# A Fourier layer with a two-layer MLP: one batch's middle stage scheduled over 42 slots in place of 44

## Chip, cores, metric

One core of a Trainium2 chip. The time is that of the device for one execution, in microseconds (us); lower is better. PE is the matrix engine, DVE the vector engine, ACT the scalar engine, SPq the queue in which the sync engine issues transfers; PEld in the profile is PE's loading of weights, POOL the GpSimd engine. A "look" is one profiled execution. A transfer has "landed" when the last update of its semaphore is recorded.

## The reference, cut

```python
def _attn_ref(x, w_r, w_i, b_r, b_i):            # x: 8 x 3008 x 256
    X = np.fft.rfft(x, axis=1)
    Xr, Xi = X.real, X.imag
    Yr = Xr @ w_r - Xi @ w_i + b_r
    Yi = Xr @ w_i + Xi @ w_r + b_i
    # soft threshold of both by 0.01
    Yr = np.sign(Yr) * np.maximum(np.abs(Yr) - 0.01, 0.0)
    Yi = np.sign(Yi) * np.maximum(np.abs(Yi) - 0.01, 0.0)
    return np.fft.irfft(Yr + 1j * Yi, n=3008, axis=1)

def _moe_ref(x, w_in, w_out, s, b):              # x: 24064 x 256, hidden 2048
    r = np.maximum(x @ w_in, 0.0)
    return (s * (r * r) + b) @ w_out
```

## The kernel before

The transform of length 3008 = 94 x 32 is done as matmuls: a first DFT over 94 ("s1", the row DFT), a second over 32, the complex mix, the inverse over 32 (these three are "s23"), and a last DFT over 94 ("s4"). Batch 0 goes alone. Each later batch is woven into the MLP of earlier ones: the MLP runs slot by slot, and a plan says which unit of the transform is issued in which slot.

```python
    def schedule(start, span, units):
        for i, u in enumerate(units):
            plan.setdefault(start + (i * span) // len(units), []).append(u)
    ...
    schedule(24, 44, s23_units(1))               # 44 units: one to a slot, 24 to 67
    schedule(mark[1] - 14, 12, s4_units(1))      # mark[1] = 96: slots 82 to 93
    for b in range(2, B):
        s0, s1, s2 = mark[b - 2], mark[b - 1], mark[b]
        p = s1 - s0
        schedule(s0 + 40, p - 48, s1_units(b))   # batch 2: slots 40, 43, ... 85
        ...
    for ti in range(ti_n + 1):
        nxt = second_mms(ti - 1) if ti else []
        per_slot = -(-len(nxt) // MC)
        for mc in range(MC):                     # a slot
            if ti < ti_n:
                for u in plan.pop(ti * MC + mc, []):
                    u()
                first_mm(ti, mc)                 # 2 matmuls of 512 columns into psh (L761)
            for u in nxt[mc * per_slot : (mc + 1) * per_slot]:
                u()                              # 4 matmuls of 256 columns into psa (L832)
```

All transform units share two PSUM banks, the pool `psf`:

```python
        def fwd_unit(i):     # second DFT: 4 matmuls (L598), copy to xf, sum of its halves (L604)
        def sum_unit(h):     # 4 matmuls on that sum (L613)
        def mix_unit(i):     # 4 matmuls (L627), then 4 DVE operations, first L632 reads the bank
        def inv_unit(i):     # 2 matmuls (L657), copy to v
            ...
            if i % 2 == 1:   # two units' v go to DRAM
                nc.sync.dma_start(out=vd[2 * i - 2 : 2 * i + 2]..., in_=v)      # L666
            if i == H - 1:   # the whole comes back turned: vs, in two halves
                ...
                    nc.sync.dma_start(out=t..., in_=vv[...])                     # L673
        # s1 unit: one matmul of 512 columns (L562); s4 unit: 5 matmuls of 96 (L710) on vs
```

The built order is that of a scheduler, which may move a unit within or just over its slot. Copies out of PSUM go to DVE (line L164) or ACT (L160) by a running total of their loads. In the profile `u` and `us` are the row DFT's result on its way to DRAM and back, `xf` the second DFT's, `yt` the last DFT's; `rt` and `gt` are the MLP's hidden values before and after squaring, `ost` is an output tile.

## Time and profile before

| | before |
|---|---|
| three runs, us | 852.54, 853.90, 854.17 |
| span of the profiled run | 851.2 us |
| PE busy | 834.2 us, 98% |
| DVE, ACT busy | 82%, 76% |
| PE clock granted | 1.000 |

The lines of this profile stand in the prediction below. A line of the order of time reads: start in us, duration in us, engine, source line, operation, output <- inputs, shape, how many in a row, and in brackets how long the engine was idle before it and what ended that.

A **stall** is the time from one matmul's start to the next one's, less 0.4225 ns for each column of the first (the rate of an undisturbed stream, where 512 columns take 0.216 us); only stalls over 0.1 us are counted. The **main stretch** runs from the first to the last L832 matmul, some 787 us; it leaves out the start, where inputs are loaded. It was 788.58 us in this profile. The first expectations below count from the first L598 matmul of batch 1 instead (779.6 us in this profile); where that matmul isn't moved, the main stretch is 8.95 us longer.

### The profile page before, as it was taken

The numbers are of one execution on the slowest core, as the hardware profiler recorded it, in microseconds if no ns is written. First come the engines' busy times: TensorE is split into PE (matmuls) and PEld (weight loads), VectorE is DVE, ScalarE is ACT, GpSimd is POOL, SyncE is SP. The second block draws the span as 40 slices with busy tenths as digits, with TensorE's granted clock in tenths as the row PEclk, the third lists the DMA queues.
The fourth block names the chain that finished last, engine by engine and source line by source line (L and its number), as shares of the span: only waits on it lengthen the run. The fifth ranks groups of instructions, "written<-read, shape, count | busy, mean of one in ns | idle before, by whom it ended". The sixth has DMA issues, their size and how long they took to land.

```text
span 851.2 us, 17087 instructions
## 1 busy us (share of the span) xinstructions
PE 834.2 (98%) x6645; PEld 598.4 (70%) x6645; DVE 697.7 (82%) x1025; ACT 642.9 (76%) x858; POOL 47.2 (6%) x72
## 2 busy tenths in 40 slices
PE   7899999999999999999999999999999999999997
PEld 6757776777677766777667776777667777766765
DVE  6898987888878887888878888888977888776674
ACT  5897787788778887787777887787877787766673
POOL 5421000000000000000000000000000000000000
PEclk9999999999999999999999999999999999999999
DMA  7937457424672357324662247613354233411111
GB/s 168 157 100 161 105 139 178 120 76 98 159 200 60 90 150 191 113 78 99 165 176 75 75 106 192 178 38 94 101 156 118 57 83 98 112 33 38 38 44 50
DMA packets 105458, 95.07 MB, mean 112 GB/s; under 512 B 9510, under 2 KB 97578, under 8 KB 104034
## 3 DMA queue, kind: packets, MB, share of 16 engines
q1 hardware_dynamic: 98930, 79.57, 32.5%
q0 software_dynamic: 6448, 14.42, 10.5%
q8 instruction: 52, 0.85, 0.4%
q14 instruction: 28, 0.23, 0.1%
HBM read 52.54 MB, written 46.66 MB: 117 GB/s over the span
## 4 chain that ended last, share of the span: by engine, by line
PE 87%; DVE 4%; ACT 3%; DMA 3%; issue 1%; POOL 0%; DVEq 0%; ACTq 0%; SPq 0%; POOLq 0%
PE psa L832 36%; PE psh L761 35%; PE psf L627 4%; PE psf L562 2%; PE psf L598 2%; PE psf L613 2%; PE psf L710 2%; PE psf L657 2%; DVE gt L775 1%; ACT rt L768 1%; DMA x<-in_x_dram 1%; DMA vs<-vd 1%; DMA vd<-v 1%; PE psh L410 1%; DMA out_dram<-ost 0%
## 5 line engine op out<-in xcount | busy, mean ns | idle before, releaser
L768 ACT ACTIVATE rt<-psh 128x1024 f32<-128x1024 f32 (+2 forms) x384 | 387.1, 1009 | 116.8 <-PE psh L761 115.6
L775 DVE TENSOR_TENSOR gt<-rt 128x1024 f16<-128x1024 f32 (+2 forms) x323 | 386.6, 1200 | 98.4 <-ACT rt L768 97.9
L832 PE MATMUL psa<-w_out_t,gt 128*128 128x256 f16 (+1 forms) x3024 | 454.5, 272 | 0.1
L832 PEld LDWEIGHTS <-gt 128*128 128x128 f16 (+1 forms) x3024 | 301.0, 101 | 187.5 <-issue 1.7
L761 PE MATMUL psh<-yt,w_in 128*128 128x512 f16 (+1 forms) x1344 | 396.6, 378 | 0.3 <-ACT rt L768 0.3
L761 PEld LDWEIGHTS <-w_in 128*128 128x128 f16 x1536 | 142.7, 98 | 27.7 <-issue 2.7
L842 DVE SCALAR_TENSOR_TENSOR ost<-psa,s_bc,bias_bc 128x512 f32<-128x512 f32 (+2 forms) x97 | 71.1, 733 | 8.3 <-PE psa L832 6.9
L772 ACT ACTIVATE gt<-rt 128x1024 f16<-128x1024 f32 (+2 forms) x61 | 64.0, 1050 | 0.9
L632 DVE TENSOR_TENSOR ring<-psf,s 128x512 f16<-128x512 f32 x84 | 57.5, 685 | 4.3 <-PE psf L627 4.0
L160 ACT CAST v<-psf 128x512 f16<-128x512 f32 x78 | 45.4, 582 | 19.4 <-PE psf L657 19.4
L160 ACT CAST xf<-psf 128x512 f16<-128x512 f32 x83 | 48.6, 586 | 11.1 <-PE psf L598 11.1
L160 ACT CAST u<-psf 96x512 f16<-96x512 f32 x81 | 46.9, 581 | 11.9 <-PE psf L562 11.6
L761 PE MATMUL psh<-tail,w_in 128*128 128x512 f16 (+1 forms) x192 | 52.1, 353 | 0.0
L627 PE MATMUL psf<-W_g,xf 128*128 128x256 f16 x336 | 50.4, 273 | 0.0
L160 ACT CAST yt<-psf 128x480 f16<-128x480 f32 (+2 forms) x74 | 37.4, 517 | 14.7 <-PE psf L710 14.7
L189 POOL DMA_DIRECT2D x<-in_x_dram x36 | 18.9, 531 | 430.9 <-PE psf L562 430.0
L562 PE MATMUL psf<-x,A_t 94*96 94x512 f16 x104 | 39.6, 381 | 1.9 <-ACT yt L160 0.5
L638 DVE TENSOR_TENSOR ring<-ring,high 128x512 f16<-128x512 f16 x84 | 35.5, 423 | 2.1
L639 DVE TENSOR_TENSOR ring<-ring 128x512 f16<-128x512 f16 x84 | 35.5, 423 | 2.0
L637 DVE TENSOR_TENSOR ring<-ring,low 128x512 f16<-128x512 f16 x84 | 35.4, 422 | 1.6
L627 PEld LDWEIGHTS <-xf 128*128 128x128 f16 x336 | 32.9, 98 | 3.7
L710 PE MATMUL psf<-C_t,vs 96*128 96x96 f16 x448 | 32.9, 205 | 0.9 <-DMA vs<-vd 0.9
(89 smaller groups left out, 495.8 us busy)
## 6 DMA issues: line engine op xcount, KB each, us to landing
out_dram<-ost SPq DMA_DIRECT2D x152, 128.0 KB
ud<-u SPq DMA_DIRECT2D x28, 384.0 KB
us<-ud SPq DMA_DIRECT2D x28, 384.0 KB
vd<-v SPq DMA_DIRECT2D x42, 256.0 KB
vs<-vd SPq DMA_DIRECT2D x14, 768.0 KB
x<-in_x_dram POOLq DMA_DIRECT2D x28, 376.0 KB, 6.0
ring<-ring SPq DMA_DIRECT2D x280, 32.0 KB
out_dram<-ost SPq DMA_DIRECT2D x16, 120.0 KB
```

The lines of the kernel that those rows point to most:

```text
L160: return None, nc.scalar.copy(out=dst, in_=src)
L562: nc.tensor.matmul(ps[0:96, :], A_t[0:N1, :], x16[(b, c)][0:N1, j * D : (j + 2) * D], start=True, stop=True,)
L627: nc.tensor.matmul(ps[:, r, :], xt[:, 2 - r, dc], W_g[:, dc, r], start=(dc == 0), stop=(dc == DC - 1),)
L632: nc.vector.tensor_tensor(out=t, in0=ps, in1=hold[i // 2][:, i % 2].unsqueeze(1).to_broadcast([P, 2, D]), op=ALU.add,)
L638: nc.vector.tensor_tensor(out=m, in0=m, in1=high, op=ALU.min)
L710: nc.tensor.matmul(ps[:, j * 96 : (j + 1) * 96], vs[(b, h)][:, k, ec * P : (ec + 1) * P], C_t, start=True, stop=True,)
L761: nc.tensor.matmul(o, w_in_t[dc][:, mc * P : (mc + 1) * P], r, start=(dc == 0), stop=(dc == DC - 1),)
L768: nc.scalar.activation(out=rt[:, :, 0:w], in_=ps[:, :, 0:w], func=AF.Relu)
L772: nc.scalar.activation(out=gt[:, :, 0:w], in_=rt[:, :, 0:w], func=AF.Square)
L775: nc.vector.tensor_tensor(out=gt[:, :, 0:w], in0=rt[:, :, 0:w], in1=rt[:, :, 0:w], op=ALU.mult)
L832: nc.tensor.matmul(ps[0:size, h, :], gts[(ti, mc // 2)][:, mc % 2, sub * size : (sub + 1) * size], w_out_t[:, mc, :], start=(mc == 0), sto ...
L842: nc.vector.scalar_tensor_tensor(out=ost[0:size, 0:k], in0=ps[0:size, 0:k], scalar=s_bc[0:size], in1=bias_bc[0:size, 0:k], op0=ALU.mult, o ...
```

## The change

The intent: let the last inverse of batch 1 come two slots earlier, so that its result is back from DRAM when the last DFT needs it.

```diff
-    schedule(24, 44, s23_units(1))
+    schedule(24, 42, s23_units(1))
     schedule(mark[1] - 14, 12, s4_units(1))
```

## The prediction

> **What bounds the kernel now.** I read the page first, then the sum of PE's waits, then the order of time around the two places that the change touches. The page and its row of slices:
>
> ```profile
> PE 834.2 (98%) x6645; PEld 598.4 (70%) x6645; DVE 697.7 (82%) x1025; ACT 642.9 (76%) x858; POOL 47.2 (6%) x72
> PE   7899999999999999999999999999999999999997
> PEclk9999999999999999999999999999999999999999
> ```
>
> PE is busy for 98% of the span at full clock, and only the first slices and the last fall short. All PE idle time is 851.2 - 834.2 = 17.0 us. The view of waits, restricted to PE from 60 to 140 us, which holds all of batch 1's second DFT, mix and inverse, has one entry:
>
> ```profile
> PE psf L710 <- DMA vs<-vd: 0.9, 1, 0.9
> ```
>
> That is the first matmul of the last DFT of batch 1, which needs `vs`, reloaded from DRAM after the inverse has stored `vd`. The order of time there, first PE, then the queue of the sync engine:
>
> ```profile
> 133.90 0.57 PE L761 MATMUL psh<-yt,w_in 128*128 128x480 f16 x2
> 134.30 0.60 PE L832 MATMUL psa<-w_out_t,gt 128*128 128x256 f16 x4
> 135.79 0.60 PE L710 MATMUL psf<-C_t,vs 96*128 96x96 f16 x10 [0.89 <-DMA vs<-vd]
> ...
> 118.91 1.86 SPq L787 DMA_DIRECT2D out_dram<-ost  x2
> 120.87 3.21 SPq L666 DMA_DIRECT2D vd<-v  x2
> 129.12 0.79 SPq L673 DMA_DIRECT2D vs<-vd  x2
> ```
>
> Without the wait the last DFT would have come at 134.30 + 0.44 = 134.74, so it costs 135.79 - 134.74 = 1.05 us of PE's stream (0.89 is what remains after the modelled end of the matmuls before it). The last inverse unit is issued at 120.15, so the way from it to the landed `vs` is 135.75 - 120.15 = 15.6 us, and PE offers 134.74 - 120.15 = 14.6 us of other work. The shortfall is the wait.
>
> How long is a slot, the unit of the schedule? It is two matmuls of 512 columns into `psh` and four of 256 into `psa`. From 67.22 to 68.09 below, such a block takes 0.87 us: 0.43 for the pair, 0.44 for the four. A DFT unit (four of 128) takes 0.22, a sum or mix unit 0.44, an inverse unit 0.22.
>
> ```profile
> 67.00 0.39 PE L598 MATMUL psf<-F_t,us 128*128 128x128 f16 x4
> 67.22 0.59 PE L761 MATMUL psh<-yt,w_in 128*128 128x512 f16 x2
> 67.23 0.74 DVE L842 SCALAR_TENSOR_TENSOR ost<-psa,s_bc,bias_bc 128x512 f32<-128x512 f32 x1
> 67.66 0.60 PE L832 MATMUL psa<-w_out_t,gt 128*128 128x256 f16 x4
> 67.89 1.21 DVE L775 TENSOR_TENSOR gt<-rt 128x1024 f16<-128x1024 f32 x1
> 68.09 0.39 PE L598 MATMUL psf<-F_t,us 128*128 128x128 f16 x4
> 69.02 0.48 DVE L604 TENSOR_TENSOR xf<-xf 128x256 f16<-128x256 f16 x2
> 69.36 0.61 PE L613 MATMUL psf<-W_t,xf 128*128 128x256 f16 x4
> ```
>
> This is the head of the stage: DFT 0, one block, DFT 1, one block, sum 0. The sum unit needs both `xf` additions of the vector engine (L604), and these stand behind a `gt` that runs to 69.10. So it starts at 69.36, already 0.18 us after PE was ready (68.75 + 0.43).
>
> **What the Trainium skill says.** "TensorE: Matmul & The Clock Gate", section "Back-to-back issue gap", gives N / 2.4 + 2.5 ns between warm matmuls: 216 ns at 512 columns, 109 at 256. The trace agrees: 0.43 us a pair and 0.44 us four. So PE has no slack inside a block, and only waits can be won. "DMA: Bandwidth & Descriptors", section "Two DMAs through the same engine are not ordered", has the issuing engine wait for the completion of a write before it issues a read of the same bytes. The trace agrees: the sync queue sits from 124.1 to 129.1 us between the store of `vd` and the load of `vs` (the view of that queue's waits has 4.9 us), so an earlier last inverse moves the whole chain. "DVE: scalar operands, raw-bit mode, write accounting and state across instructions", section "Flops that outlive an instruction", calls the vector engine's queue one in-order queue. The trace agrees: the two additions start at 69.02 together, right behind `gt`, though the first `xf` had been copied by 68.27.
>
> **The change part by part.** There are 44 units (12 DFT, 6 sum, 12 mix, 12 inverse, 2 empty). Over 44 slots they lie one to a slot, 24 to 67. Over 42 slots they lie in 24 to 65, and two slots hold two: slot 24 (DFT 0 and 1) and slot 45 (inverse 2 and DFT 9). No instruction is added or removed on PE. The evacuation helper keeps running totals and sends a few copies elsewhere: over the program the order of instructions shows `u` copies on the vector engine 27 in place of 23, `yt` and `gt` squarings three fewer, and the scalar engine takes two more squarings. From about a third of the program on both engines' orders are the same to the end. So the tail is not touched.
>
> Part 1, the `vs` wait. The last inverse comes two slots earlier, so 2 x 0.87 = 1.74 us more of other work lies behind it: 14.6 + 1.7 = 16.3 us against the 15.6 needed. The wait goes, with 0.7 us to spare: -1.05 us. In the sync queue the store of the last-but-one `v` now also stands ahead of two stores of `ost` (1.86 us), which gives a little more room.
>
> Part 2, the head. DFT 0 and 1 are now issued at 67.00 and 67.22. In the built order sum 0 follows after the 512-column pair and three of the four 256-column matmuls: PE is ready at 67.44 + 0.43 + 0.33 = 68.20. The vector engine's order there is unchanged (`ost`, `gt`, two additions), and neither `ost` nor `gt` depends on a DFT unit, so the additions still come at 69.02 and sum 0 at 69.36. The stall is 69.36 - 68.20 = 1.16 us in place of 0.18: +0.98 us.
>
> Part 3, waits for the two `psf` banks in 91 to 121 us. I compared start to start of all matmuls with 0.4225 ns a column, and found six stalls above 0.1 us there: 0.12 + 0.31 + 0.19 + 0.19 + 0.26 + 0.31, together about 1.4 us. The pattern behind the 0.31 at 94.33 is a mix, then a block, an inverse, and at once a third user of `psf`, whose bank the vector engine still reads (L632 from 93.60 to 94.28). In the new order this comes back once, as DFT 9 behind inverse 2 in slot 45. The burst at the end (inverse 8 to 11 with row-DFT units of batch 2 between) has one such unit in place of two. I put the new sum at about 1.1 us: -0.3 us, with an uncertainty of 0.5.
>
> Sum: -1.05 + 0.98 - 0.3 = about -0.4 us, so 853.9 - 0.4 = 853.5 us.
>
> **The rivals.** First, the head's stall is smaller than I say, if the vector engine reaches the additions sooner, or if the scalar engine does not queue. For it: a wait of 1 us is unusual in this kernel after 60 us. Against it: the order of the vector engine is the same and its times there come from `ost` and `gt`. Then the gain is near -1.3, and the time 852.6. Second, a new wait takes the place of the removed one: the vector engine is busy for 14.2 of 15 us from 85 to 100 us, and the same work in two slots less delays `psf` banks. For it: that share of 0.95 is the highest of all stretches that I read. Against it: the head's stall gives the vector engine back a microsecond first. Each lost bank costs 0.3 us, so three of them make it 854.4. Third, the transfer is not hidden: the DMA engines are busy for 0.97 to 1.09 of the time from 130 to 136 us, and a stronger overlap with the load of `x` at 126.99 would stretch `vs`. Then part of the 1.05 stays, and the time is 854.0 to 854.6.
>
> **Range and chances.** All terms are near 1 us and two of them cancel. Their spread is some 0.7 us and the three runs of before differ by 1.6 us (852.54 to 854.17). I take 852.0 to 855.2 for 8 in 10. A change of 2% is 17 us, more than all waits of the stage together, and as much as all idle time of PE: faster 0.01, slower 0.01, within 2% 0.98.
>
> **What would show it right or wrong.** Step 1: no wait of PE L710 for `vs` near 135 us, and the load issued earlier relative to the first last-DFT matmul. Step 2: a gap of about 1 us before the first L613, with the two additions at 69.0 behind `gt`. Step 3: the stalls of L562, L598 and L657 for banks between 90 and 122 us adding up to 0.6 to 1.6 us. After 150 us the two traces should run parallel. If the gap at 69 us is missing, step 2 is wrong; if the later batches differ by more than 0.5 us, the moved copies matter more than I allow.

## The result

In the first job the changed kernel took 851.91 us (median of 6, 851.16 to 853.40), the one before 854.90 us (6 runs, 852.54 to 856.12). The ratio is 0.9969, with a 95% interval of 0.9952 to 0.9986. A ratio is the mean time of one kernel's fast runs over that of the other's of the same rounds, so not quite the ratio of these medians. By the 2% rule it is the same time; the small gain is clear of the noise in this job. The profiled run's span is 849.4 us, 1.8 less than before.

The page's busy times after the change:

```profile
PE 835.0 (98%) x6645; PEld 600.5 (71%) x6645; DVE 697.0 (82%) x1027; ACT 643.2 (76%) x856; POOL 46.6 (5%) x72
```

The view of PE's waits from 60 to 145 us has no entry any more. The order of time around the store of `vd` and the load of `vs`, after the change:

```profile
116.27 0.37 SPq L666 DMA_DIRECT2D vd<-v  x1
117.83 1.32 SPq L787 DMA_DIRECT2D out_dram<-ost  x2
119.60 0.78 SPq L666 DMA_DIRECT2D vd<-v  x1
125.11 0.80 SPq L673 DMA_DIRECT2D vs<-vd  x2
...
133.48 0.97 ACT L768 ACTIVATE rt<-psh 128x960 f32<-128x960 f32 x1 [0.66 <-PE psh L761]
133.71 0.59 PE L710 MATMUL psf<-C_t,vs 96*128 96x96 f16 x10
134.34 1.02 ACT L160 CAST yt<-psf 128x480 f16<-128x480 f32 x2
134.55 0.27 PE L832 MATMUL psa<-w_out_t,gt 128*128 128x256 f16 x1
134.95 0.38 PE L562 MATMUL psf<-x,A_t 94*96 94x512 f16 x1
```

The load of `vs` is issued at 125.1 us instead of 129.1, and its first half has landed at 130.64, by the record of its semaphore; PE comes to it at 133.71 and finds it there. The next thing to see is at 134.95: PE could have started this L562 at 134.66, but its `psf` bank is one that the copies of `yt` are just emptying, a stall of 0.29 us. ACT was still at L768 when the first five L710 were done. In the profile before, PE stood still for a microsecond in front of L710, ACT had ended its L768 meanwhile, and the copies were not late:

```profile
136.21 1.02 ACT L160 CAST yt<-psf 128x480 f16<-128x480 f32 x2 [0.74 <-PE psf L710]
```

Part of the wait that went has come back as a wait for a bank. The head of the stage, after the change:

```profile
66.71 0.61 PE L598 MATMUL psf<-F_t,us 128*128 128x128 f16 x8
67.16 0.59 PE L761 MATMUL psh<-yt,w_in 128*128 128x512 f16 x2
67.59 0.60 PE L832 MATMUL psa<-w_out_t,gt 128*128 128x256 f16 x4
67.60 1.21 DVE L775 TENSOR_TENSOR gt<-rt 128x1024 f16<-128x1024 f32 x1
68.03 0.59 PE L761 MATMUL psh<-yt,w_in 128*128 128x512 f16 x2
68.46 0.49 PE L832 MATMUL psa<-w_out_t,gt 128*128 128x256 f16 x3
68.73 0.48 DVE L604 TENSOR_TENSOR xf<-xf 128x256 f16<-128x256 f16 x2
69.07 0.61 PE L613 MATMUL psf<-W_t,xf 128*128 128x256 f16 x4
```

Both DFT units are issued together (x8), then a whole block and most of a second one, and only then the sum unit L613. The stall there is 69.07 - (68.46 + 0.33) = 0.28 us, not the 1.16 predicted.

Stalls in the two profiles, us:

| place | before | after |
|---|---|---|
| head (first L613) | 0.18 | 0.29 |
| `psf` banks, 72 us to the last DFT | 1.37 | 0.51 |
| first L710, wait for `vs` | 1.05 | 0 |
| last DFT of batch 1, behind it | 0 | 0.58 |
| everything later | 3.18 | 3.03 |
| main stretch | 788.58 | 787.10 |

The stalls fall by 1.37 us together; the rest of the 1.48 us lies in differences below 0.1 us each.

From 350 us on, the L832 matmuls of the two traces lie the same distance apart, 1.76 to 1.77 us, to the end: the copies that moved between DVE and ACT (the last of them near 244 us) cost nothing later. Of this distance 0.29 us arose before the first L832, where both kernels are the same.

### The profile page after: what moved, and what is told of

Same layout as the page of the kernel before. It is cut to its first block, busy times and chain, and to the rows that moved or that the text cites. A ratio compares the mean times of both kernels' runs of the same rounds, so it can differ in the third digit from the quotient of the medians.

```text
span 849.4 us, 17085 instructions
## 1 busy us (share of the span) xinstructions
PE 835.0 (98%) x6645; PEld 600.5 (71%) x6645; DVE 697.0 (82%) x1027; ACT 643.2 (76%) x856; POOL 46.6 (5%) x72
## 4 chain that ended last, share of the span: by engine, by line
PE 88%; DVE 4%; ACT 3%; DMA 2%; issue 1%; POOL 0%; SPq 0%; DVEq 0%; ACTq 0%; POOLq 0%
PE psa L832 36%; PE psh L761 36%; PE psf L627 4%; PE psf L562 2%; PE psf L613 2%; PE psf L598 2%; PE psf L657 2%; PE psf L710 2%; ACT rt L768 1%; DVE gt L775 1%; DMA x<-in_x_dram 1%; DMA out_dram<-ost 1%; PE psh L410 1%; ACT yt L160 0%; ACT vs L160 0%
## 5 line engine op out<-in xcount | busy, mean ns | idle before, releaser
L768 ACT ACTIVATE rt<-psh 128x1024 f32<-128x1024 f32 (+2 forms) x384 | 387.1, 1009 | 119.1 <-PE psh L761 117.7
L832 PE MATMUL psa<-w_out_t,gt 128*128 128x256 f16 (+1 forms) x3024 | 454.3, 272 | 0.1
L832 PEld LDWEIGHTS <-gt 128*128 128x128 f16 (+1 forms) x3024 | 300.9, 101 | 187.2 <-issue 1.7
L772 ACT ACTIVATE gt<-rt 128x1024 f16<-128x1024 f32 (+2 forms) x63 | 66.2, 1050 | 1.0
L160 ACT CAST u<-psf 96x512 f16<-96x512 f32 x77 | 44.5, 580 | 11.0 <-PE psf L562 10.7
L562 PE MATMUL psf<-x,A_t 94*96 94x512 f16 x104 | 39.7, 381 | 1.7 <-ACT yt L160 0.5
L710 PE MATMUL psf<-C_t,vs 96*128 96x96 f16 x448 | 33.0, 205 | 0.1
```

The lines of the kernel that those rows point to most:

```text
L160: return None, nc.scalar.copy(out=dst, in_=src)
L562: nc.tensor.matmul(ps[0:96, :], A_t[0:N1, :], x16[(b, c)][0:N1, j * D : (j + 2) * D], start=True, stop=True,)
L710: nc.tensor.matmul(ps[:, j * 96 : (j + 1) * 96], vs[(b, h)][:, k, ec * P : (ec + 1) * P], C_t, start=True, stop=True,)
L768: nc.scalar.activation(out=rt[:, :, 0:w], in_=ps[:, :, 0:w], func=AF.Relu)
L772: nc.scalar.activation(out=gt[:, :, 0:w], in_=rt[:, :, 0:w], func=AF.Square)
L832: nc.tensor.matmul(ps[0:size, h, :], gts[(ti, mc // 2)][:, mc % 2, sub * size : (sub + 1) * size], w_out_t[:, mc, :], start=(mc == 0), sto ...
```

## The experiments

Three theories after the result. A: the gain is in the kernel, as the table has it, and every entry repeats. B: the waits scatter from run to run. C: the measured 0.3% is mostly scatter in the start, where inputs are loaded.

### The kernel before, once more

No edit; five rounds against itself.

> The kernel before, unchanged, against itself. Theory A (the difference is in the kernel: the vs wait and waits for psf banks): ratio 1.000 within 0.002, and in the trace the stretch from the first L598 matmul of batch 1 to the last L832 matmul is again 779.6 us within 0.2, with the vs wait of 0.9 us and bank waits in the same places. Rival B (waits scatter from run to run): the vs wait or the bank waits between 90 and 122 us move by more than 0.3 us. Rival C (the measured 2.6 us is mostly scatter outside of this stretch): the span differs by up to 2 us from 851.2 with the stretch unchanged, by the loads before 20 us.

Measured: 853.52 us (852.02 to 855.83), ratio 1.0011 (0.9995 to 1.0028); main stretch 787.72 us. All six bank stalls are where they were, and sum to 1.37 us again. But the wait for `vs` is gone:

```profile
120.28 1.28 SPq L666 DMA_DIRECT2D vd<-v  x2
127.25 0.79 SPq L673 DMA_DIRECT2D vs<-vd  x2
134.68 0.59 PE L710 MATMUL psf<-C_t,vs 96*128 96x96 f16 x10
```

Sync queue and PE, as above. Here the first half of `vs` landed at 134.59, and PE came at 134.68: just in time, in the very program that had waited 1.05 us. So theory A is wrong for this entry and right for the banks, and the wait for `vs` is a race that PE sometimes loses. I had built on one execution. With this I went on with theory A2: what the order fixes repeats, and the `vs` wait is drawn anew in each execution.

### The last DFT one slot later

```diff
-    schedule(mark[1] - 14, 12, s4_units(1))
+    schedule(mark[1] - 13, 12, s4_units(1))
```

> Before, with the last DFT of batch 1 one slot later and its units left where they were (44 slots): only the vs wait is touched. Theory A: the wait falls by one block, from 1.05 to about 0.2 us, and some 0.3 us come back as a bank wait in the last DFT; stretch 779.6 - 0.6 = 779.0 us, bank waits in 90 to 122 us as before (1.4 us). Rival B (the vs wait alone is what the change gains): the stretch falls by 0.85. Rival D (the wait does not matter): 779.6.

Measured: 852.46 us (851.02 to 852.90), ratio 0.9988 (0.9974 to 1.0002); main stretch 787.63 us, bank stalls 1.38, `vs` stall 0.62 us. It could not tell the theories apart: one slot of more time, and yet 0.62 us of wait, because in this execution `vs` landed 16.2 us after the last inverse (15.6 in the first profile, 14.5 in the second). Nor did it touch the `vs` wait alone, as I had expected: the stalls after 150 us fell from 3.18 to 2.63 us. The traces show that some copies after 136 us went to the other engine, and that PE's built order differs in three places from 239 to 310 us.

### All units two slots earlier, none doubled

```diff
-    schedule(24, 44, s23_units(1))
+    schedule(22, 44, s23_units(1))
```

> Before, all 44 units moved two slots earlier, still one to a slot: same end as 42 slots, no doubled slots. Theory A: vs wait gone (-1.05), about +0.4 back in the last DFT; head 0.2 us; bank waits depend on how the units meet the row-DFT units of batch 2, which in the built order is like that of the change (one inverse followed by a row-DFT unit straight after a mix), so 0.5 to 0.9 us instead of 1.4: stretch 778.0 to 778.7. Rival E (the gain in bank waits needs the doubled slots): bank waits stay at 1.4 and the stretch is 779.0.

Measured: 852.21 us (850.96 to 853.62), ratio 0.9992 (0.9977 to 1.0006). The expectation's stretch, counted from the first L598, is 779.23 us, which isn't comparable, as that matmul now comes two slots earlier; I had overlooked it. By the main stretch, 786.44 us, it is the shortest of all. No `vs` wait (landed 2.6 us before PE came), head 0.12, bank stalls 0.21, last DFT 0.29. So the smaller sum of bank stalls needs no doubled slots: rival E falls. I took it to come from how batch 1's units meet the row-DFT units of batch 2; the next run moves these.

### Row DFT of batch 2 one slot later

```diff
-        schedule(s0 + 40, p - 48, s1_units(b))
+        schedule(s0 + (41 if b == 2 else 40), p - 48, s1_units(b))
```

> Before, with the row-DFT units of batch 2 one slot later and all else left: only their meeting with batch 1's units changes. Theory A: the vs wait stays at about 1.0 us, the bank waits of 1.4 us in 90 to 122 us change by at least 0.4 us either way (the order has two inverses followed by such a unit right after a mix, as before): stretch 779.0 to 780.0, with the difference in L562 and L657 and nowhere else. Rival B (compression alone made the bank waits fewer): 1.4 us again, 779.6.

Measured: 851.98 us (851.60 to 852.75), ratio 0.9990 (0.9977 to 1.0003); main stretch 787.39 us. The bank stalls moved, from six places to three (0.39 and 0.45 us before an L562, 0.35 before an L657), but their sum fell by only 0.19 us, to 1.18: less than the 0.4 expected. A stall before an L598 went as well, 0.18 us came in the last DFT, and the later stalls are 3.03 us as with 42 slots, so it was not L562 and L657 alone. There was no `vs` wait in this look, with a landing 12.2 us after the last inverse. So moving the row-DFT units moves the stalls, and the size has to be read from the order each time. The meeting alone isn't shown as the cause: with the units, copies from 91 to 244 us went to other engines too.

### The changed kernel, once more

No edit.

> The changed kernel (42 slots), unchanged, against the kernel before. Theory A2, after the first look at the kernel before again (bank waits are fixed by the order, the vs wait is a race that PE loses in some executions): bank waits in 72 to 132 us again 0.51 us, head 0.29, last DFT 0.3 to 0.6, no vs wait, and vs landed at least 2 us before PE comes to it; from the first to the last L832 matmul 787.1 us within 0.3. In time, the bank waits and head are worth -0.75 us, the last DFT +0.3 to +0.6, the vs wait 0 to -1.5: ratio 0.9980 to 0.9995. Rival C2 (the first measured ratio of 0.9969 is the kernel's own): 0.9975 or less again.

Measured: 852.04 us (851.24 to 853.52), ratio 0.9983 (0.9965 to 1.0002). Main stretch 787.10 us, as in the first look, with head 0.29, banks 0.51, last DFT 0.58, and no `vs` wait: landed at 132.18, PE at 135.08. Rival C2 isn't excluded by the interval, but the point lies where A2 puts it.

### The kernel before, third and fourth look

No edit; one look each.

> Third look at the kernel before. Theory A2: bank waits 1.37 us at the same places to 0.02 us; the first half of vs lands 14 to 16.5 us after the last inverse (15.5 and 14.4 in the two looks so far), so the vs wait lies anywhere from 0 to 1.5 us. Rival F (the first look is the rule and the second the exception): 0.9 to 1.1 us.

> Fourth look at the kernel before: the same expectation as for the third. If the third and fourth both wait under 0.2 us the wait is worth under 0.5 us in the mean; if both wait about 1 us, it is worth 0.8.

Measured: 853.32 and 854.25 us (state unknown, single runs); main stretches 788.24 and 789.84 us; bank stalls 1.38 in both, in the same six places. The `vs` stall was 0.73 us in the third and 2.33 us in the fourth, more than I had allowed. Of the fourth, the sync queue and PE:

```profile
118.96 2.25 SPq L787 DMA_DIRECT2D out_dram<-ost  x2
121.31 1.82 SPq L666 DMA_DIRECT2D vd<-v  x2
128.86 0.79 SPq L673 DMA_DIRECT2D vs<-vd  x2
137.12 0.60 PE L710 MATMUL psf<-C_t,vs 96*128 96x96 f16 x10 [2.17 <-DMA vs<-vd]
```

The load was issued earlier than in the first profile (128.86 against 129.12) and yet landed 1.3 us later: both the queue and the transfer itself vary. The four looks together: 1.05, 0, 0.73 and 2.33 us, 1.03 in the mean.

### The last stores of `vd` from another queue

```diff
-                nc.sync.dma_start(
+                (nc.scalar if b == 1 and i >= 9 else nc.sync).dma_start(
                     out=vd[2 * i - 2 : 2 * i + 2].rearrange("q p e -> p q e"), in_=v
                 )
```

> Before, with the last two stores of vd of batch 1 issued by the scalar engine; the order of PE is unchanged and the sync engine's differs in these two alone. Theory G (vs is late because both of these stores stand behind two stores of ost in the sync queue): they are issued within 1 us of their copies, vs lands 11.5 to 13.5 us after the last inverse, the vs wait is 0 in the profile; some 0.3 us come back as a bank wait in the last DFT, and issuing costs the scalar engine up to 1 us, which may lengthen bank waits near 120 us by up to 0.5. From the first to the last L832 matmul 787.2 to 788.0. Rival H (the transfers themselves take this long, whatever the queue): 14 us or more.

Measured: 853.85 us (4 runs, 853.00 to 854.37), ratio 1.0003 (0.9983 to 1.0023); main stretch 787.71 us. PE's order is unchanged and so are its bank stalls (1.38 us); no `vs` wait, and 0.29 us back in the last DFT. Queue of ACT, then of the sync engine:

```profile
119.94 0.39 ACTq L666 DMA_DIRECT2D vd<-v  x1
122.11 0.37 ACTq L666 DMA_DIRECT2D vd<-v  x1
...
127.88 0.80 SPq L673 DMA_DIRECT2D vs<-vd  x2
```

Each store takes 0.37 to 0.39 us to issue here, and goes right after its copy. `vs` landed at 133.53, 12.5 us after the last inverse (121.08), inside the range of theory G and outside that of H. But G is not shown by it: in the run with the row DFT one slot later both stores stood in the sync queue, behind two stores of `ost`, and `vs` landed even sooner, after 12.2 us. The time of the four runs shows no gain; what it should gain in the mean, about 0.9 us (788.60 less 787.71), is inside its interval. Where the time goes is told apart below, over all looks.

### Two combinations

First the two helpful parts together, then an edit that was meant to move the later batches' row-DFT units as well:

```diff
-    schedule(24, 44, s23_units(1))
-    schedule(mark[1] - 14, 12, s4_units(1))
+    schedule(22, 44, s23_units(1))
+    schedule(mark[1] - 13, 12, s4_units(1))
# the second of the two, in addition:
-        schedule(s0 + 40, p - 48, s1_units(b))
+        schedule(s0 + (40 if b == 2 else 41), p - (48 if b == 2 else 49), s1_units(b))
```

> Both parts that helped: all 44 units two slots earlier, one to a slot, and the last DFT of batch 1 one slot later. Theory A2: no vs wait (vs landed 2.7 us ahead with the units alone earlier, so 3.5 us here), bank waits 0.21, head 0.12, and the 0.29 us in the last DFT gone, since in the built order no row-DFT unit stands in the slot of the doubled first unit any more: from the first to the last L832 matmul 786.44 - 0.29 = 786.15 us, within 0.3; ratio to before 0.996 to 0.9985. Rival: the last DFT one slot later meets the next tile's first matmul, which reads its result, and loses 0.3 or more there: 786.5 or more.

Measured: 852.05 us (850.88 to 853.64), ratio 0.9983 (0.9960 to 1.0005); main stretch 787.72 us, 1.6 more than expected. Up to the last DFT all came as expected: head 0.12, banks 0.22, `vs` 0, last DFT 0. But the stalls of later batches rose from 3.03 to 4.78 us. The largest is a race of the same kind in a later batch; from the view of PE's waits:

```profile
PE psf L598 <- DMA us<-ud: 0.6, 1, 0.6
```

It is 0.81 us start to start. The other 0.94 us, a net sum, are bank stalls, some at new places. Two things changed there with the moved units: copies after 137 us went to other engines, and PE's built order differs from that of the shift in four places from 309 to 539 us, though the plan there is the same. I have tried neither alone.

> The one before this, with the row-DFT units of batches 3 to 7 one slot later and spread by one slot less dense. Theory A2 (bank waits come from who meets whom in a slot, in every batch): the waits of L562 after 150 us, about 2.3 us in the kernel before, change by more than 0.5 us; from the order I expect fewer, 785.0 to 786.0. Rival: the collisions only move, 786.2 or more.

Measured: 851.72 us (851.10 to 853.51), ratio 0.9976 (0.9953 to 1.0000); main stretch 786.79 us. No wait for `us` in this look. The later stalls are 3.75 us: 4.78 less the 0.81 us of that wait and less 0.21 us of one bank stall (an L657 near 298 us) that went. All the others are where they were. But this run can't decide between the theory and the rival, for its edit doesn't do what I meant. `schedule` puts unit i of 16 into slot start + (i * span) // 16, rounded down. With the start one later and the span one less, only the first unit of each of the five batches comes a slot later; the other fifteen stay in their slots. PE's order accordingly differs from the first combination's in 20 of 6645 matmuls. What moving the later row-DFT units would do stays untested. Neither combination has a shorter main stretch than the plain shift.

### The shift and the change, side by side

No edits beyond those above.

> The 44 units two slots earlier, one to a slot, once more, beside the 42 slots: the shortest first-to-last L832 so far (786.44 us). Theory A2: everything that the order fixes repeats: 786.4 us within 0.1 unless a load of us or vs comes late, no vs wait. In time the 0.7 us against 42 slots are below what these runs can tell: ratio to before 0.997 to 0.9995.

> Third look at the 42 slots. Theory A2: 787.10 us again within 0.05 from the first to the last L832 matmul, vs landed 2.5 to 3.5 us before PE comes to it; ratio to before 0.9970 to 0.9995. Rival (two equal looks were luck, the race is there with 42 slots too): a vs wait of 0.3 us or more.

Measured on one chip, with the same 9 runs of the kernel before (853.33 us): the shift 850.97 us (850.81 to 852.11), ratio 0.9978 (0.9964 to 0.9991), main stretch 786.44 us again; the 42 slots 851.14 us (850.92 to 851.94), ratio 0.9978 (0.9965 to 0.9990), main stretch 787.11 us again. `vs` landed 3.0 and 2.2 us before PE came. So the third look at 42 slots has no wait either, and the two equal looks were not luck, as far as a third can tell. The shift is 0.66 us shorter in the traces; the runs can't tell the two apart.

All looks at the two kernels, from the records of semaphores and starts in the traces. "Issue" is from the last inverse to the issue of the last store of `vd`, "store" from there to its landing, "load" from the issue of the first half of `vs` to its landing; "landed" is from the last inverse to the end of all that, "PE there" to the first L710 as it would come without a wait:

| kernel, look | issue | store | load | landed | PE there | `vs` stall | main stretch |
|---|---|---|---|---|---|---|---|
| 44 slots, 1 | 2.48 | 6.42 | 6.63 | 15.60 | 14.59 | 1.05 | 788.58 |
| 44 slots, 2 | 1.03 | 6.07 | 7.34 | 14.50 | 14.59 | 0 | 787.72 |
| 44 slots, 3 | 1.85 | 6.92 | 6.44 | 15.27 | 14.59 | 0.73 | 788.24 |
| 44 slots, 4 | 1.77 | 6.83 | 8.21 | 16.87 | 14.59 | 2.33 | 789.84 |
| 42 slots, 1 | 1.91 | 5.45 | 5.53 | 12.95 | 16.02 | 0 | 787.10 |
| 42 slots, 2 | 1.91 | 5.28 | 5.87 | 13.12 | 16.02 | 0 | 787.10 |
| 42 slots, 3 | 1.92 | 5.85 | 6.00 | 13.84 | 16.03 | 0 | 787.11 |

The queue is not what differs: the mean "issue" is 1.8 us with 44 slots and 1.9 with 42. The two transfers are each over 1 us shorter with 42, in the mean of these looks; the two looks at the plain shift, with landings after 13.4 and 13.1 us, go with them. Why they are shorter is open: other transfers are under way beside them, in another mix in each kernel, and I have no run that takes these away. Nor is it sure in each execution: in the second of the two combinations, with the order of stores as with 42 slots, `vs` landed after 16.1 us (in the first, 13.5, by the same program up to there). It cost nothing there, as the last DFT came after 17.1 us.

## Why the prediction was right or wrong

**The whole.** The class (within 2%) was right. The predicted 853.5 us was too high by 1.6 against the first job's 851.91, which lies a tenth of a microsecond below the range's lower end; later jobs gave 852.04 and 851.14. Put together, all 54 timed runs of the kernel before have a mean of 853.54 us (851.59 to 858.95), all 17 of the changed one 851.87 us (850.92 to 853.52): -1.67 us. The main stretch says the same: the mean of four looks, 788.60, less 787.10 is -1.50 us. Against the one look at the kernel before that had no wait (787.72), 0.62 us of this is left: so much is in the order of the program, and the rest is the mean of a wait drawn four times. The prediction had -0.4.

**Part 1, the `vs` wait: right in kind, and its size a draw.** It went, as said. The -1.05 was one execution's value; the wait ranges from 0 to 2.33 us in four looks, and their mean, 1.03, equals it by chance. The margin was mis-sized: predicted 0.7 us, measured 3.1, 2.9 and 2.2. PE's side was near (16.0 us of work, 16.3 predicted). On the other side I had taken 15.6 us as fixed, with "a little more room" from the order of the sync queue; it fell to 13.0, 13.1 and 13.8 us, and in the transfers, not in the queue; why is open. So the last inverse's two slots would have removed two of the three waits by themselves (16.0 us against 15.3 and 15.6) and all but 0.85 us of the third (16.87). That the race is never lost with 42 slots isn't shown: three looks had no wait, but one landing of 16.1 us in a near kernel is just over what 42 slots offer.

**Part 2, the head: the step that failed.** Predicted +0.98, measured +0.11. "Sum 0 follows after the 512-column pair and three of the four 256-column matmuls" is a misreading of the built order: there are two pairs between, a whole block and then most of another. The scheduler had held the sum unit back. The rest of the step held: the two additions start behind `gt`, at 68.73 after the change, which is the same distance from the stage's start as before, 2.02 us, and this fixes the sum unit; two blocks less one matmul fill the time that I thought empty.

**Part 3, the banks: right in sign, too small.** Predicted -0.3, measured -0.86 (1.37 to 0.51, under the 0.6 to 1.6 that I had set as the sign of being right), and it repeats to 0.01 us in every look, so it is a sure part of the gain. The predicted 1.1 us was 0.59 too much. Some 0.31 of this is inverse 2 with DFT 9 behind it, for which I copied a stall that didn't come. The other 0.28 lie in the small stalls of 0.12 and twice 0.19 us that I had kept: 0.10 and 0.14 are left, and why isn't shown. (I had also counted 27 `u` copies on DVE in place of 23; the traces have 32 in place of 28, and one `xf` copy more.) The pattern of inverse 2, in the profile before and then in the one after:

```profile
93.60 0.68 DVE L632 TENSOR_TENSOR ring<-psf,s 128x512 f16<-128x512 f32 x1
93.81 0.38 PE L657 MATMUL psf<-ring,T_t 128*128 128x256 f16 x2
94.33 0.38 PE L562 MATMUL psf<-x,A_t 94*96 94x512 f16 x1
```

```profile
92.00 0.69 DVE L632 TENSOR_TENSOR ring<-psf,s 128x512 f16<-128x512 f32 x1 [0.54 <-PE psf L627]
92.59 0.38 PE L657 MATMUL psf<-ring,T_t 128*128 128x256 f16 x2
92.81 0.39 PE L598 MATMUL psf<-F_t,us 128*128 128x128 f16 x4
```

Before, DVE reads the mix's bank from 93.60 to 94.28, 0.4 us after it could have, because a `gt` and an addition stood ahead in its queue; L562 waits for it. After, DVE is idle when the mix ends, has read the bank by 92.69, and L598 at 92.81 doesn't wait. Much the same neighbours on PE, another state of the reader. The Trainium skill's "DVE: scalar operands, raw-bit mode, write accounting and state across instructions", section "Flops that outlive an instruction", with its one in-order queue of the DVE, agrees with both.

**Not foreseen: the last DFT.** With the wait gone its copies come late, and 0.29 us or, with 42 slots, twice 0.29 us are lost there. The first of the two comes with the removal of the wait, not with the 42 slots: the kernel before shows 0.29 as well in the look without a wait, and 0 in the three with one, and so does the plain shift. The second, near 141.5 us, shows with 42 slots alone.

**The rivals.** A smaller stall at the head was the first and came true, for a reason that I hadn't given. A new wait in place of the old came true in small: 0.58 us, though behind the last DFT and not in the stretch from 85 to 100 us that was named. A longer transfer by contention did not: the transfers became shorter.

**Theory C** holds in part: the first job's -0.31% is more than the traces have (-1.5 us is -0.18%), and the other two jobs gave -0.17% and -0.22%. The first L832 comes anywhere from 57.8 to 60.6 us in 14 traces, though no kernel changes anything before it: the start alone scatters by 2.8 us.

## What to carry to other kernels

A wait for a transfer, read from one profile, is one draw: look at the unchanged kernel three or four times before a number is built on it. Give such a race a margin of more than its spread, and expect part of a removed wait to come back from the engines that had rested in it. Waits for shared buffers follow the order and repeat to a hundredth of a microsecond, so these can be judged from one trace, even where timed runs can't see them. And before a run, print the slots that an edit really gives: a start of one more with a span of one less moved one unit in sixteen here.

## What the Trainium skill lacked or had wrong

- "DMA: Bandwidth & Descriptors", section "Issuing engines are not separate DMA queues", calls the sequencer's time to initiate a transfer "usually small relative to the DMA itself". Here the issue of batch 1's last store of `vd` (256 KB) took from 0.44 to 1.45 us on the sync queue in four looks at one program, beside 6.1 to 6.9 us from its start to its landing: up to 23%, and not the same in two executions. The page has no such spread.
- No section that I read gives the scatter of a chain of store, wait and load: 14.5 to 16.9 us over four looks at one program.
- "TensorE: Matmul & The Clock Gate", section "Back-to-back issue gap", gives a sustained 131 ns a matmul at 512 columns for a stream with weight loads, beside 216 ns by its formula, which it calls that of an isolated matmul (the prediction cites the formula without this). Here each of these matmuls has its own weight load (6645 of each), and a pair takes 0.43 us, 216 ns each: the formula holds, the lower figure is not reached.
